# An attention and mixture-of-experts kernel: the same operations in another searched order

## The chip, the cores and the metric

The kernel runs on one core of a Trainium2 chip. The metric is the device time of one execution in microseconds (us); of several executions the median is given. The core has five engines with an instruction stream each: PE (TensorE, matrix products into PSUM), DVE (VectorE), ACT (ScalarE), POOL (GpSimd) and SP (SyncE, which here issues the loads and stores). Transfers between HBM and the on-chip memory are moved by 16 DMA engines that all streams share.

## The reference

The input x holds 4 batches of 11456 tokens with 128 channels. Two attention steps with 32 inducing points give every token a mixture of 32 vectors, and a top-1 mixture of 8 experts follows.

```python
def mab(q, kv):
    s = scale * (q @ kv.transpose(0, 2, 1))
    a = np.exp(s - s.max(-1, keepdims=True))
    a /= a.sum(-1, keepdims=True) + 1e-09
    return a @ kv
h = mab(I, x)          # 32 rows for each batch
x = mab(x, h)          # a mixture of these rows for each token
...
logits = x @ w_gate    # 8 experts, the largest is taken
h = np.maximum(xe @ w1[e], 0.0)
out[mask] = gate_w[mask, None] * (h @ w2[e])
```

## The kernel before

A batch is cut into 6 groups, so there are 24 tiles of 960 KB, numbered k = 6 x batch + group. A tile is loaded once (LT, L728) and stays on the chip until it has been used twice. The first use belongs to the step that makes h: scores against the inducing points (S1, L740), their largest (M1, L743), exponentials (E1, L780), and the product with the tokens themselves in another layout (H, L793). That layout is either loaded (LN, L731) or made by transposing the tile on PE (TR, L751) and copying it out of PSUM on ACT or DVE (TE, L759 or L761).

When a batch's h is there, one expert is assumed for the whole batch, taken from its mean row. DVE computes the row index of that expert's matrices (pick, L841 to L844), ACT reads the index and fetches both matrices with one transfer of 1 MB (fetch, L852 and L853, names GA0 to GA3). The gate product G (units, L880) and the product P (second, L902) read them and give h4, the 32 output rows of that batch. One buffer holds the matrices, so a fetch waits until P of the batch before has read them.

The second use of a tile: scores against h (S2, L740), exponentials (E2, L981), gate logits of four tiles at a time (LG, L985) with a chain of small DVE operations and one exponential (PR, L1026), spreading of the gate (SP, L1041), weighing (W, L1044), the product with h4 in four quarters (X, L1048), a copy of each quarter out of PSUM on ACT or DVE (V, L759 or L761), and one store of the tile by SP (OUT, L734). The four copies of a tile must be done before its store. Tile 22 is stored in two halves.

At the end a scalar, nleft, is computed (count_left, L1055 to L1060). Every engine reads it (L1164), and only if it isn't zero a general part follows that treats each token by its own expert (not entered here).

The order of all this is not written by hand. `make_plan` lists the operations with what each depends on, the buffers it takes, and a rank; `schedule` (L114 on) plays the engines through in time and gives each free engine the ready operation with the lowest rank. The instructions are then issued in that order, and on the chip each engine keeps to it. The rank of an operation is a sum of three numbers from the table PLAN, and the same table names for some copies the engine (ACT or DVE) that has to make them:

```python
r = plan[table][at] + off.get(what, 0) + own.get(name, 0)
```

The fetch and the store are such operations (w is the buffer of the matrices, ix the pick, vs the four copies of a tile):

```python
ga = gc = op(f"GA{b}", ("C", b, "GA"), {"ACT": (1300, 1300)}, lambda w=w, b=b: K.fetch("ACT", w, b, 0, 2 * F), [ix], take=[w], dma=("ACT", 1048576, 8192, 2400, 1300))
op(f"OUT{name}", ("X", k, "OUT"), {"SP": (400, 400)}, lambda ob=ob, b=b, g=k % NG, lo=lo, hi=hi: K.store(ob, b, g, lo, hi), vs[lo:hi], use=[ob], dma=("SP", P * size, size, 1000, LAG))
```

A tile in memory is one of 19 buffers named big, a bank of PSUM is named bank, and the numbers behind these names in the rows below tell one buffer from another.

Of the kernel before, what the change touches and what calls it, by code (L numbers as in the profile page):

```python
# [19 lines left out]
P = 128  # L20
# [15 lines left out]
SWITCH, STICK, INFLIGHT, BEHIND = 145, 11437, 3, 15731  # L36
# [77 lines left out]
def schedule(ops, caps, groups):  # L114
# [54 lines left out]
    while done < len(ops):  # L169
# [83 lines left out]
        22576, -215, 14169, 28949, 16135, 34517, 14097, 191, 4002, 6426, 7963, -6317, 10900, 1498, 8024, -8116, 8452,  # L253
        -538, 10545, -12557, 2397, -23157, 10591, 16643,
    ],
    "L": [
        -29189, -20072, -22138, -25158, -35332, -21900, -37208, -31064, -25285, -35121, 5583, 8561, 12852, 1863,
        -4529, 16988, 4272, 5407, 14400, 6829, 17850, 29121, 33456, 31071,
    ],
    "N": [  # L260
        12772, 4341, -2376, 6450, 8539, 16120, -6122, -27329, -2958, 18930, -18049, -32917, -14840, 13704, -18266,
        3276, 12274, 10466, -10433, -30560, 12476, 19786, 30172, 37075,
    ],
    "S": [
        10068, 9798, -1298, -1286, -4892, -6897, -23049, -13916, -26910, -16934, -10574, 2427, -23263, -49482, 8229,
        -28059, 34705, -41524, 1858, 4084, 16975, -13970, 16003, 35169,
    ],
    "R": [
        -22198, -46069, -31967, -57874, -57432, 2945, -46313, -34100,
    ],  # L270
    "X": [
        3851, -21673, -61781, 13591, -13346, -23064, -23010, -4543, 1213, -60388, -39796, -45518, -11840, 8412,
        -27893, -41405, -19426, -45032, -29697, 7754, -3754, -15221, -20520, -12592,
    ],
    "C": [
        4574, -20912, -62733, -11069,
    ],
    "off": {
# [7 lines left out]
    },  # L286
    "own": {
# [1101 lines left out]
```

## Time and profile before

| | us |
|---|---|
| median of 3 runs | 163.82 (163.63 to 164.72) |
| the profiled execution, its own time | 162.93 |
| the profiled execution, span from the first to the last instruction | 161.1 |
| PE busy | 142.5 |
| DVE busy | 123.8 |
| ACT busy | 95.7 |
| moved by DMA in the span | 61.74 MB |

Three stages follow each other and overlap: loads (until about 90 us), stores (from about 90 us on), and a last part in which no engine computes while the remaining stores are moved. Times in the rows are counted from the start of the span. A row of the windows gives busy time and, in brackets, the number of instructions of PE, PEld (weight loads), DVE, ACT and POOL, then PE's granted clock, the busy share of the DMA engines and the rate that they moved. The rate and the busy share of the DMA engines have to be read together: an engine counts as busy while a packet is under way, however long it takes.

### The profile page before, as it was taken

To read this page: it belongs to the slowest core of one execution; us is meant where nothing else is said; L and a number is where in the kernel's file an instruction comes from. 1 tells how busy PE (TensorE), PEld (TensorE's weight loads), DVE (VectorE), ACT (ScalarE), POOL (GpSimd) and SP (SyncE) were. 2 spreads that over 40 slices of the span, in tenths; PEclk is the share of its full clock that TensorE was granted. 3 is DMA by queue.
4 is the path that set the end of the run, shared out by engine and by line. 5 is a ranking of instruction groups with operands and counts; after the bars stand their busy time and mean duration, and the time that the engine had idled before them with its cause. 6 is when DMAs were issued, how large, how long until landed. Compare 5 with 4: busy or idle time off the path is not lost.

```text
span 161.1 us, 4956 instructions
## 1 busy us (share of the span) xinstructions
PE 142.5 (89%) x1980; PEld 85.1 (53%) x1981; DVE 123.8 (77%) x351; ACT 95.7 (59%) x197; POOL 10.3 (6%) x59
## 2 busy tenths in 40 slices
PE   7999899999999999999999999999999967994100
PEld 4385665866974753495855764654543232471100
DVE  2046669864969999999999899999999999994000
ACT  3074751725804545796857884896986988667000
POOL 1100000000001011001000011002010000102000
PEclk9999999999999999999999999999999999999555
DMA  5999999999799999999999879999999999999991
GB/s 154 429 420 430 420 422 422 419 417 417 268 375 405 373 422 422 425 415 427 414 430 421 337 320 416 323 369 408 401 350 280 428 423 420 425 427 417 432 371 39
DMA packets 9389, 61.74 MB, mean 383 GB/s; under 512 B 1040, under 2 KB 1168, under 8 KB 8848
## 3 DMA queue, kind: packets, MB, share of 16 engines
q1 hardware_dynamic: 8640, 57.10, 86.7%
q10 hardware_dynamic: 720, 4.26, 7.5%
q8 instruction: 17, 0.28, 0.7%
q14 instruction: 12, 0.10, 0.2%
HBM read 37.76 MB, written 23.59 MB: 381 GB/s over the span
## 4 chain that ended last, share of the span: by engine, by line
PE 76%; DVE 9%; DMA 4%; ACT 2%; issue 1%; POOL 1%; SPq 0%; DVEq 0%
PE bank L740 25%; PE bank L751 15%; PE bank L793 13%; PE bank L1048 13%; DMA big<-in_xT 4%; PE bank L704 3%; PE bank L1041 3%; PE bank L985 3%; DVE mid L1044 2%; ACT big L759 2%; DVE big L761 1%; PE bank L902 1%; PE bank L880 1%; DVE mid L1037 1%; POOL thr_all L968 1%
## 5 line engine op out<-in xcount | busy, mean ns | idle before, releaser
L759 ACT COPY big<-bank 128x480 f32<-128x480 f32 (+2 forms) x121 | 60.2, 594 | 26.7 <-PE bank L751 20.4
L1048 PE MATMUL bank<-mid,h 32*128 32x480 f32 x192 | 32.9, 596 | 2.2 <-DVE mid L1044 1.7
L751 PEld LDWEIGHTS bank<-ident,big 128*128 128x128 f32 x210 | 22.7, 141 | 8.9 <-ACT big L759 3.3
L751 PE MATMUL bank<-ident,big 128*128 128x128 f32 x210 | 26.0, 276 | 0.7 <-ACT big L759 0.7
L740 PE MATMUL bank<-big,csb 128*32 128x480 f32 (+2 forms) x200 | 24.6, 554 | 0.4 <-DMA big<-in_xT 0.4
L793 PE MATMUL bank<-big,mid 128*32 128x129 f32 x720 | 24.5, 274 | 0.0
L743 DVE TENSOR_REDUCE mx<-bank 128x1 f32<-128x480 f32 x24 | 15.4, 651 | 11.4 <-PE bank L740 9.9
L793 PEld LDWEIGHTS bank<-big,mid 128*32 128x32 f32 x720 | 21.3, 110 | 4.6 <-issue 2.9
L1048 PEld LDWEIGHTS bank<-mid,h 32*128 32x128 f32 x192 | 15.6, 183 | 13.5 <-ACT big L759 5.9
L981 ACT ACTIVATE mid<-bank,nb 128x480 f32<-128x480 f32 x24 | 15.4, 661 | 11.6 <-DVE nb L976 6.1
L761 DVE COPY big<-bank 128x480 f32<-128x480 f32 (+2 forms) x31 | 19.4, 649 | 2.9 <-PE bank L751 2.0
L740 PE MATMUL bank<-big,hc 128*32 128x480 f32 x192 | 21.5, 568 | 0.0
L780 ACT ACTIVATE mid<-bank,mx 128x480 f32<-128x480 f32 x24 | 15.1, 662 | 7.0 <-DVE mx L777 4.0
L783 DVE STREAM_TRANSPOSE mid<-mid 128x480 f32<-128x480 f32 x24 | 15.3, 656 | 0.8 <-ACT mid L780 0.7
L972 DVE TENSOR_REDUCE mx<-bank 128x1 f32<-128x480 f32 x24 | 15.1, 642 | 0.1
L1044 DVE TENSOR_TENSOR mid<-mid,bank 128x480 f32<-128x480 f32 x24 | 14.7, 634 | 0.2
L1041 PE MATMUL bank<-mid,sel 32*128 32x480 f32 x48 | 13.7, 594 | 0.0
L740 PEld LDWEIGHTS bank<-big,hc 128*32 128x32 f32 x192 | 6.3, 110 | 8.4 <-issue 6.6
L740 PEld LDWEIGHTS bank<-big,csb 128*32 128x32 f32 x200 | 5.9, 110 | 6.4 <-issue 3.0
L1041 PEld LDWEIGHTS bank<-mid,sel 32*128 32x128 f32 x48 | 5.0, 183 | 3.1 <-issue 1.2
L985 PE MATMUL bank<-mid,gzb 128*32 128x480 f32 x48 | 6.0, 570 | 0.0
L700 PE MATMUL bank<-ones 128*128 128x384 f32 x8 | 4.9, 792 | 1.1 <-DVE ones L682 1.1
(100 smaller groups left out, 111.2 us busy)
## 6 DMA issues: line engine op xcount, KB each, us to landing
big<-in_xT SPq DMA_DIRECT2D x23, 960.0 KB, 14.0
out<-big SPq DMA_DIRECT2D x23, 960.0 KB, 7.1
big<-in_xn SPq DMA_DIRECT2D x10, 967.5 KB, 9.9
wt<-in_w ACTq DMA_DIRECT2D x4, 1024.0 KB, 9.8
out<-big SPq DMA_DIRECT2D x2, 480.0 KB, 7.2
big<-in_xT SPq DMA_DIRECT2D x1, 512.0 KB, 3.8
big<-in_xT SPq DMA_DIRECT2D x1, 448.0 KB, 9.8
csb<-in_consts ACTq DMA_DIRECT2D x1, 66.5 KB, 4.0
```

Of the source, the lines that this page charges most:

```text
L740: self.nc.tensor.matmul(self.blk(ps[32 * q : 32 * q + 32, 32 * lo : 32 * hi]), lhsT=lhsT, rhs=x[:, lo:hi, q, :], start=True, stop=True)
L743: self.nc.vector.tensor_reduce(self.mx1[b][g // 2][:, g % 2 : g % 2 + 1], self.bank(fe)[:, :GW], AX.X, ALU.max)
L751: self.nc.tensor.transpose(ps[:, k * P : (k + 1) * P], x[:, k0 + k].rearrange("p q t -> p (q t)"), self.ident)
L759: self.nc.scalar.copy(dst, src)
L761: self.nc.vector.tensor_copy(dst, src)
L780: self.nc.scalar.activation(self.at(e), self.bank(fe)[:, :GW], AF.Exp, bias=self.mx1[b][p + 1][:, 2:3], scale=SCALE)
L783: self.nc.vector.transpose(self.at(e), self.at(e))
L793: self.nc.tensor.matmul(ps[32 * j : 32 * j + 32, : P + 1], lhsT=e[:, k, :], rhs=x[:, k, :], start=(n < 4), stop=(n >= 2 * GB - 4))
L981: self.nc.scalar.activation(self.at(e), self.bank(fe)[:, :GW], AF.Exp, bias=self.nb2[r][:, u : u + 1])
L1041: self.nc.tensor.matmul(self.bank(s)[:, :GW], lhsT=self.sel[rows], rhs=self.at(lv)[rows], start=True, stop=True)
L1044: self.nc.vector.tensor_tensor(out=self.at(e), in0=self.at(e), in1=self.bank(s)[:, :GW], op=ALU.mult)
L1048: self.nc.tensor.matmul(self.bank(o)[:, :GW], lhsT=self.h4[b][rows], rhs=self.at(e)[rows], start=True, stop=True)
```

## The change

The table PLAN has other numbers throughout, two constants of the planner are different, and the lists that fix an engine for some copies are different. The operations, their dependencies, the buffers and the tile sizes are the same. The file grows by 3 lines, so a line number behind the table is 3 higher after the change (L853 is L856).

```diff
-SWITCH, STICK, INFLIGHT, BEHIND = 145, 11437, 3, 15731
+SWITCH, STICK, INFLIGHT, BEHIND = 145, 11302, 3, 13971
...
 PLAN = {
     "A": [
-        22576, -215, 14169, 28949, 16135, 34517, 14097, 191, 4002, 6426, 7963, -6317, 10900, 1498, 8024, -8116, 8452,
+        2385, -1402, 28311, 13134, 33635, 6526, 1078, 21421, 8652, 5804, 12112, -2541, 14024, -7580, 6532, -10203,
...
```

The order was searched with an added charge for stores issued close behind a fetch of expert matrices; that charge is not in the file, only the table that came of it. The lists that fix an engine now name 37 copies for DVE (31 before); in the last stage, behind the logits of tiles 16 to 19, DVE makes 12 copies of outputs where it made 10.

ACT at the fourth fetch (GA3), before the change. The copies of tile 5 go to big_94, those of tile 4 to big_104:

```order
L759 COPY big_95<-bank_79 128x480
L759 COPY big_104<-bank_81 128x480
L759 COPY big_94<-bank_82 128x480
L759 COPY big_94<-bank_84 128x480
L759 COPY big_104<-bank_83 128x480
L759 COPY big_94<-bank_85 128x480
L852 TENSOR_LOAD ii_223
L852 ISA x2
L853 ISA
L853 DMA wt_130<-in_w 128x2048
L759 COPY part_231<-bank_81 128x128
L759 COPY big_104<-bank_86 128x480
```

The same place after the change. Here tile 4 is in big_88 and tile 5 in big_104:

```order
L762 COPY big_88<-bank_85 128x480
L1029 ACTIVATE mid_120<-mid_120 128x60x7
L762 COPY big_104<-bank_84 128x480
L762 COPY big_88<-bank_80 128x480
L762 COPY big_104<-bank_79 128x480
L762 COPY big_104<-bank_86 128x480
L855 TENSOR_LOAD ii_223
L855 ISA x2
L856 ISA
L856 DMA wt_130<-in_w 128x2048
L762 COPY part_231<-bank_81 128x128
L762 COPY big_104<-bank_83 128x480
```

The last copy of tile 4 moved from behind the fetch to ahead of it, with two copies between; the last copy of tile 5 moved from ahead of the fetch to behind it. SP's stores of the two tiles changed places with them.

PE where the gate product of the first pick is made (L704 on csb and hs_208, which the first fetch waits for through DVE), before the change. A row of L740 with hc is the product of scores of one tile in the second use, L793 is one H:

```order
L751 MATMUL bank_83<-ident,big_100 128x128 x3
L740 MATMUL bank_82<-big_99,hc_185 32x480 x4
L704 MATMUL bank_81<-csb,hs_208 32x8 x4
L704 MATMUL bank_81<-csb,hT_all 32x8 x4
L704 MATMUL bank_84<-mq_0_153,fold 32x8 x4
```

The same place after the change:

```order
L754 MATMUL bank_79<-ident,big_99 128x128 x4
L707 MATMUL bank_82<-mq_0_153,fold 32x8 x4
L743 MATMUL bank_81<-big_100,hc_185 32x480 x4
L743 MATMUL bank_85<-big_104,hc_185 32x480 x4
L743 MATMUL bank_84<-big_93,csb 32x480 x4
L743 MATMUL bank_80<-big_94,hc_185 32x480 x4
L743 MATMUL bank_79<-big_87,hc_185 32x480 x4
L796 MATMUL bank_83<-big_95,mid_116 32x129 x15
L707 MATMUL bank_82<-csb,hs_208 32x8 x4
L707 MATMUL bank_82<-csb,hT_all 32x8 x4
```

The pick's products moved behind five products of scores and one H, where they stood behind one product of scores. The user of the fetched matrices, G (L880, now L883), has two products of scores fewer ahead of it than before.

SP at the end, before the change (three full stores behind the two halves of tile 22):

```order
L734 DMA out<-big_90 128x960 x2
L734 DMA out<-big_87 128x1920
L734 DMA out<-big_100 128x1920
L734 DMA out<-big_92 128x1920
L1164 TENSOR_LOAD nleft
```

And after the change:

```order
L737 DMA out<-big_102 128x960 x2
L737 DMA out<-big_93 128x1920
L1167 TENSOR_LOAD nleft
L1167 ISA x2
L737 DMA out<-big_99 128x1920
L737 DMA out<-big_97 128x1920
```

The read of nleft moved from behind all stores to ahead of the last two. On DVE the count (now L1058 to L1063) stands ahead of the last two copies, where it stood behind all of them.

At the start, SP's first transfer is now the whole tile 0; before it was the first half of tile 6, which is now second.

## Rows read from the trace of the kernel before

**Rows 1.** The page, part 2: rate of the DMA engines in 40 slices.
```profile
GB/s 154 429 420 430 420 422 422 419 417 417 268 375 405 373 422 422 425 415 427 414 430 421 337 320 416 323 369 408 401 350 280 428 423 420 425 427 417 432 371 39
```

**Rows 2.** Timeline of the tail, DVE: start us, us, line, operation, idle before.
```profile
148.64 0.17 DVE L1055 TENSOR_TENSOR sure<-low_all,thr_all 128x6 f32<-128x6 f32 x1 [1.24 <-POOL thr_all L968]
...
149.88 0.16 DVE L1060 TENSOR_SCALAR nleft<-bank 128x1 int32<-128x1 f32 x1 [0.68 <-PE bank L1059]
```

**Rows 3.** Windows, two long stretches.
```profile
48.00:124.00 76.00, 76.00 (x1153) 43.34 (x1155) 72.97 (x222) 54.91 (x113) 6.68 (x27) 1.00 0.98 388
124.00:144.00 20.00, 17.29 (x141) 8.12 (x135) 19.44 (x47) 15.53 (x34) 0.70 (x3) 1.00 1.01 424
```

**Rows 4.** DMA issues of 104 to 117.5, 126 to 149, 118.3 to 119.9: KB, us to landing.
```profile
out<-big SPq DMA_DIRECT2D x6, 960.0 KB, 4.7
...
out<-big SPq DMA_DIRECT2D x11, 960.0 KB, 7.4
...
out<-big SPq DMA_DIRECT2D x2, 960.0 KB, 10.8
wt<-in_w ACTq DMA_DIRECT2D x1, 1024.0 KB, 9.7
```

**Rows 5.** Windows around the fourth, the third and the first fetch.
```profile
118.00:120.00 2.00, 2.00 (x36) 0.82 (x28) 1.92 (x6) 1.36 (x4) 0.33 (x2) 1.00 1.04 355
120.00:122.00 2.00, 2.00 (x19) 0.57 (x14) 1.97 (x9) 1.69 (x3) 0.22 (x1) 1.00 0.95 244
122.00:124.00 2.00, 2.00 (x26) 0.69 (x24) 2.00 (x6) 1.56 (x4) 0.00 (x0) 1.00 0.94 239
...
100.00:102.00 2.00, 2.00 (x68) 1.80 (x64) 1.96 (x9) 1.50 (x3) 0.56 (x2) 1.00 1.01 294
102.00:104.00 2.00, 2.00 (x30) 0.88 (x30) 1.93 (x5) 1.44 (x4) 0.00 (x0) 1.00 0.98 393
...
52.00:56.00 4.00, 4.00 (x96) 2.96 (x90) 3.96 (x13) 1.74 (x3) 0.37 (x2) 1.00 0.98 372
```

**Rows 6.** DMA queues in 120 to 123.5; q10 carries the fetches: packets, MB, share.
```profile
q10 hardware_dynamic: 96, 0.79, 92.2%
```

**Rows 7.** Timeline of ACT's and SP's DMA issues at the fourth, third, first fetch.
```profile
118.42 0.35 ACTq L853 DMA_DIRECT2D wt<-in_w  x1
...
118.71 1.18 SPq L734 DMA_DIRECT2D out<-big  x2
...
98.66 0.35 ACTq L853 DMA_DIRECT2D wt<-in_w  x1
...
104.44 0.33 SPq L734 DMA_DIRECT2D out<-big  x1
...
51.91 0.35 ACTq L853 DMA_DIRECT2D wt<-in_w  x1
...
52.10 0.79 SPq L728 DMA_DIRECT2D big<-in_xT  x1
```

**Rows 8.** Timeline of ACT, copies out of PSUM ahead of the fourth fetch.
```profile
112.09 2.41 ACT L759 COPY big<-bank 128x480 f32<-128x480 f32 x5
```

**Rows 9.** DMA in 56 to 60 us: all packets, then the fetches' queue.
```profile
DMA packets 224, 1.67 MB, mean 418 GB/s; under 512 B 14, under 2 KB 14, under 8 KB 111
...
q10 hardware_dynamic: 112, 0.92, 55.2%
```

**Rows 10.** Timeline of PE at the user of the first fetch (L880).
```profile
65.53 1.00 PE L740 MATMUL bank<-big,hc 128*32 128x480 f32 x8
66.33 0.63 PE L880 MATMUL bank<-wt,hT_all 128*32 128x256 f32 x8
```

**Rows 11.** The page, part 5: copies out of PSUM on DVE; busy us, mean ns.
```profile
L761 DVE COPY big<-bank 128x480 f32<-128x480 f32 (+2 forms) x31 | 19.4, 649 | 2.9 <-PE bank L751 2.0
```

**Rows 12.** SP at the end: the last two stores, and the read of nleft.
```profile
147.24 2.31 SPq L734 DMA_DIRECT2D out<-big  x2
...
L1164 SPq TENSOR_LOAD <-nleft x1: 849/849/849, 150.1 to 150.1; - x1
```

More of the change, by code (lines that the diff above doesn't have):

```diff
@@ L252 @@
     "A": [
-        22576, -215, 14169, 28949, 16135, 34517, 14097, 191, 4002, 6426, 7963, -6317, 10900, 1498, 8024, -8116, 8452,
-        -538, 10545, -12557, 2397, -23157, 10591, 16643,
+        2385, -1402, 28311, 13134, 33635, 6526, 1078, 21421, 8652, 5804, 12112, -2541, 14024, -7580, 6532, -10203,
+        7059, -2760, 9977, -13414, 2050, -23025, 10682, 16850,
     ],
     "L": [
-        -29189, -20072, -22138, -25158, -35332, -21900, -37208, -31064, -25285, -35121, 5583, 8561, 12852, 1863,
-        -4529, 16988, 4272, 5407, 14400, 6829, 17850, 29121, 33456, 31071,
+        -29755, -23396, -21084, -25190, -36575, -23093, -34252, -37352, -25092, -31089, 8881, 6270, 12370, -4707,
+        1170, 16463, 3474, 5592, 14308, 6744, 17567, 28569, 32255, 31070,
     ],
     "N": [
-        12772, 4341, -2376, 6450, 8539, 16120, -6122, -27329, -2958, 18930, -18049, -32917, -14840, 13704, -18266,
-        3276, 12274, 10466, -10433, -30560, 12476, 19786, 30172, 37075,
+        -18663, 3735, 12016, 11822, -5651, 15948, 9052, -18534, -11764, 6103, -5977, -35933, -5395, 13660, -27398,
+        17803, 3361, 9450, -16842, -30295, 12619, 20197, 31553, 37979,
     ],
     "S": [
-        10068, 9798, -1298, -1286, -4892, -6897, -23049, -13916, -26910, -16934, -10574, 2427, -23263, -49482, 8229,
-        -28059, 34705, -41524, 1858, 4084, 16975, -13970, 16003, 35169,
+        -280, -4243, -710, 9493, 17027, -7951, -13994, -28002, -24337, 1613, -12108, -17135, -25789, -50709, 7905,
+        -28776, 33975, -41739, 461, -15538, 16653, 3801, 10271, 35050,
     ],
     "R": [
-        -22198, -46069, -31967, -57874, -57432, 2945, -46313, -34100,
+        -44787, -45651, -30899, -58535, -59615, 3019, -22021, -33329,
     ],
     "X": [
-        3851, -21673, -61781, 13591, -13346, -23064, -23010, -4543, 1213, -60388, -39796, -45518, -11840, 8412,
-        -27893, -41405, -19426, -45032, -29697, 7754, -3754, -15221, -20520, -12592,
+        -11971, -2621, -60694, 3686, -13159, -22217, -22667, -4799, -345, -61467, -39936, -46315, -11898, 7638,
+        -17880, -40850, -27968, -46174, -13735, 14632, 7964, -21222, -29646, -19084,
     ],
     "C": [
-        4574, -20912, -62733, -11069,
+        3750, -22440, -63404, -10617,
     ],
     "off": {
[7 rows of a table removed]
[7 rows of a table added]
     },
     "own": {
[133 rows of a table removed]
[134 rows of a table added]
     },
     "ACT": [
[3 rows of a table removed]
[4 rows of a table added]
     ],
     "DVE": [
[3 rows of a table removed]
[4 rows of a table added]
     ],
```

295 rows, old and new, of the table PLAN are left out of this document.

## Prediction

> **What bounds the kernel now.** Read the page first. In its row of rates [rows 1] the DMA engines move 400 to 430 GB/s in most of the 40 slices; the last full number is 371 in slice 39, which ends near 157, and some bytes still move in the last one. The timeline of the tail has the last instruction that an engine computes, nleft, at 149.88 [rows 2], 11 us before the span's end. So the end is a queue of stores that drains, and a microsecond that the DMA engines lose counts whole if nothing fills it later.
>
> Then the long windows [rows 3]. From 48 to 124 us TensorE is busy 76.00 of 76 us and VectorE 72.97: compute sets the pace at which tiles become ready to store. From 124 to 144 the DMA engines run at 424 GB/s; I take that as the full rate.
>
> Then time to landing [rows 4]. The stores of 104 to 117.5 land a median 4.7 us after issue: hardly a queue. Those of 126 to 149 take 7.4, so some 2.7 us of queue stand before them. What built that queue lies between the two: the stores issued at 118.3 to 119.9 need 10.8 us.
>
> The short windows say why [rows 5]: 355 GB/s in 118 to 120, 244 and 239 in the next two. Missing against 424 are 2 x (69 + 180 + 185) = 868 KB, or 2.05 us at the full rate. The engines weren't idle: in 120 to 123.5 us the queue that carries the fetch of an expert's matrices takes 92.2% of their time [rows 6] and moves little in it. The fetch was issued by ACT at 118.42, and SP issued two stores behind it, the first at 118.71, both within 1.18 us [rows 7].
>
> Other fetches cost less. The third, issued at 98.66, has no store behind it until 104.44 [rows 7]; the windows from 100 to 104 show 294 and 393 GB/s [rows 5]: 2 x (130 + 31) = 322 KB or 0.76 us. The first, at 51.91, has one load behind it at 52.10 [rows 7]; 52 to 56 shows 372 [rows 5]: 4 x 52 = 208 KB, 0.49 us.
>
> **The change part by part.** No operation is added or removed: it is the same list, with other ranks, and with other engines for some copies out of PSUM.
>
> *The fourth fetch.* Before, ACT makes the last copy of one tile, issues the fetch, and then makes a small copy and the last copy of another tile: two stores become ready at and behind the fetch. Now the tile whose last copy stood behind the fetch gets it ahead, with two copies between, and only the other tile is completed behind. Copies on ACT go at 0.48 us each (2.41 us for five [rows 8]), so the one store should leave about 1 us ahead of the fetch, and the other about 1.1 us behind it, as the second does today.
> What is this worth? At one end nothing: 2.05 us are lost as before. At the other end the loss becomes that of the first fetch, 0.49. I take 0.76, the third's: it is the nearest in time, with stores around it and not loads, and the dearer of the two. Gain 2.05 - 0.76 = 1.29 us. It reaches the end, since the later stores stand in a queue 2.7 us deep.
>
> Here a rule of the Trainium skill speaks against the change. At 120 to 123.5 the fetch has the engines almost alone [rows 6] and moves 244 and 239 GB/s; at 56 to 60 the first fetch has 55.2% of their time, loads the rest, and 418 GB/s are moved [rows 9]. The page DMA: Bandwidth & Descriptors, section Queues, rings and completion order, says that each engine goes round-robin over the queues that have work, switching at packet boundaries. By that rule alone the bytes would take the same time whichever store stands first, so the sum would be 0 in place of 1.29; the stretch at 56 agrees with it, the one at 120 doesn't. It stands beside the first rival below.
>
> *Evictions before that fetch.* ACT has one exponential fewer ahead of the copies that began at 112.09 [rows 8], and TensorE one product of scores fewer, 0.80 us (from 65.53 to 66.33 [rows 10]). The stores of this stretch stand in no queue, so earlier ones can close small holes. At least 0, at most 0.80 us; copies of another tile come in between, so I take 0.3.
>
> *Copies moved.* VectorE gets two more copies in the last stage, at 649 ns each [rows 11], 1.30 us; ACT two fewer. What hides it is the 2.7 us queue, so I cost it at nothing; without that cover it is 1.30 us.
>
> *The count at the end.* SP now reads the scalar nleft ahead of the last two stores, and VectorE makes the count ahead of its last two copies. Queued behind SP's read are those two stores alone. Today they are issued from 147.24, over 2.31 us, so until 149.55 [rows 12]. At worst they come 1.30 (copies) + 1.40 (the count, 148.64 to 150.04 [rows 2]) + 0.85 (the read [rows 12]) later: 153.1. The engines now end about 159; with the forecast's gain they would be free for the last two stores (1.97 MB, 4.6 us at 424 GB/s) near 153. A store needs some 2.4 of its 4.7 us besides its transfer, so the worst case loses about 2.4 us, the best nothing. I take nothing: the count stands beside copies, and ACT is ahead by what VectorE takes over.
>
> *The start and the first fetch.* The first transfer is now a whole tile rather than the first half of another; TensorE has its warm-up until either can begin. I cost it at nothing, 0.3 us either way. The first gate product comes later on TensorE, and with it the first fetch. I cost that at nothing too; its price is the last rival's.
>
> Sum: 1.29 + 0.3 = 1.6 us. The profiled execution took 162.93 us, its span 161.1; that gives 161.3 for it. The median of the runs is 163.82, 0.9 above it; the same 1.6 off gives 162.2, my forecast.
>
> **The rivals.**
> *No change.* The low rate belongs to the fetch and not to what is issued near it. For it: the stores behind the fetch moved almost nothing in the bad stretch, so it isn't plain how they hurt. Against it: the first and the third fetch, of the same size, lost 0.49 and 0.76. Time: 163.82 - 0.3 = 163.5. The worst case of the count at the end, which gives the gain back, also ends near here.
> *More than forecast.* The fetch and both stores run at the full rate, and small holes close, as far as the queue of 2.7 us lets a gain through. For it: the queue is deeper than the loss that the windows show. Against it: each fetch whose rate I looked up cost something. 163.82 - 2.7 = 161.1.
> *Slower.* The first fetch comes into TensorE's path. It was issued at 51.91 [rows 7]; four products of scores at 0.80 and one sum of about that length now stand ahead of its row index, which makes it 55.9. A fetch lands 9.7 us later [rows 4], at 65.6. Its user, the product at 66.33 [rows 10], has two products fewer ahead of it, so it wants the matrices at 64.7 and is already 0.9 us late. If the low rate comes with any transfer near a fetch, the first loses 2.05 in place of 0.49 and lands at 67.2, 2.5 us late, on an engine without idle time until 124 [rows 3]; and the fourth gains nothing. 163.82 + 2.5 - 0.3 = 166.0. It decides from a lateness of 1.6 us on; below that the fourth fetch's gain outweighs it. Against it: VectorE, which works on what TensorE makes, has 3 us of idle time in that stretch [rows 3] to make good.
>
> **How the numbers follow.** Forecast 0.50, more than forecast 0.16, no change 0.20, slower 0.14. A measurement of this kernel can tell about 1% from no change, 1.64 us: faster is below 162.18, slower above 165.46. The forecast, with half a microsecond of doubt either way, lies on that bound: 0.26 of it counts as faster, 0.24 as within 1%. More than forecast is faster, 0.16; no change is within 1%, 0.20. Of the slower case 0.11 is over 1%, the rest a smaller lateness within it. That makes faster 0.42, within 1% 0.47, slower 0.11. The range goes from 160.6 (half a microsecond beyond "more than forecast") to 164.8, which takes in no change and a smaller lateness of the first fetch; the forecast's own range is 161.3 to 163.1.
>
> **What would show it.** Right: one store issued ahead of the fourth fetch and one about 1 us behind it; the windows that stood at 244 and 239 GB/s above 330; the two stores next to the fetch landing in under 9 us; the stores of 126 to 149 in about 6 us rather than 7.4. Wrong: the fetch again alone on the engines below 300 GB/s; TensorE idle before the product that reads the first fetch; the last two stores issued later than 152 with none in flight before them.

## The result and the profile after

| | before | after |
|---|---|---|
| median of 20 runs each, us | 163.88 | 164.09 |
| ratio, with its 95% interval | 1 | 1.0053 (1.0032 to 1.0073) |
| the profiled execution, us | 162.93 | 163.72 |
| its span, us | 161.1 | 161.8 |

The changed kernel is 0.5% slower by the ratio, some 0.9 us, where 162.2 us had been forecast. The medians of all runs lie only 0.2 us apart; the ratio and its interval are taken over the runs in the faster of two states, and the text goes by them. The number lies in the range; the direction is wrong.

**The fourth fetch went as forecast.** ACT's and SP's DMA issues there (timeline of the changed kernel; its line numbers are 3 higher) answer to [rows 7]:

```profile
118.70 0.33 SPq L737 DMA_DIRECT2D out<-big  x1
...
119.38 0.34 ACTq L856 DMA_DIRECT2D wt<-in_w  x1
...
120.52 0.33 SPq L737 DMA_DIRECT2D out<-big  x1
```

One store leaves 0.7 us ahead of the fetch, one 1.1 us behind it. The windows there, to be read against [rows 5] (last column GB/s):

```profile
118.00:120.00 2.00, 2.00 (x36) 0.96 (x32) 1.93 (x5) 1.83 (x6) 0.01 (x1) 1.00 1.03 416
120.00:122.00 2.00, 2.00 (x28) 0.65 (x20) 1.93 (x7) 1.80 (x4) 0.22 (x1) 1.00 1.00 407
122.00:124.00 2.00, 2.00 (x22) 0.43 (x10) 1.97 (x8) 1.08 (x2) 0.00 (x0) 1.00 1.02 328
```

Missing against 424 GB/s are 2 x (8 + 17 + 96) = 242 KB, 0.57 us, where it was 2.05. Two of the signs that had been named were missed: the window of 122 to 124 stands at 328 and not above 330, and the store behind the fetch landed after 10.1 us and not under 9. The stores of 126 to 149 land after a median 5.9 us in place of 7.4 [rows 4]:

```profile
out<-big SPq DMA_DIRECT2D x9, 960.0 KB, 5.9
```

**The first fetch came into TensorE's path.** PE's timeline at the product that reads it, before in [rows 10]; in brackets the idle time and what ended it:

```profile
63.96 1.02 PE L988 MATMUL bank<-mid,gzb 128*32 128x480 f32 x8
66.38 0.64 PE L883 MATMUL bank<-wt,hT_all 128*32 128x256 f32 x8 [1.40 <-DMA wt<-in_w]
```

The fetch was issued at 56.24 (51.91 before [rows 7]) and needed 10.1 us (ACT's timeline, then the list of DMA issues):

```profile
56.24 0.36 ACTq L856 DMA_DIRECT2D wt<-in_w  x1
...
wt<-in_w ACTq DMA_DIRECT2D x1, 1024.0 KB, 10.1
```

TensorE, which had no idle time in this stretch before, waits 1.40 us. From there on compute is late. The first weighing of a tile, on DVE, of the kernel before and of the changed one:

```profile
81.30 1.18 DVE L1044 TENSOR_TENSOR mid<-mid,bank 128x480 f32<-128x480 f32 x2
```

```profile
82.94 0.61 DVE L1047 TENSOR_TENSOR mid<-mid,bank 128x480 f32<-128x480 f32 x1
```

That is 1.64 us. What the DMA engines moved shows the balance. Three windows of the kernel before, then of the changed one (last column GB/s):

```profile
0.00:56.00 56.00, 53.79 (x820) 36.54 (x825) 36.32 (x98) 24.75 (x49) 2.99 (x25) 1.00 0.95 383
...
56.00:112.00 56.00, 56.00 (x904) 33.36 (x896) 53.57 (x167) 40.70 (x85) 4.83 (x20) 1.00 0.97 397
112.00:128.00 16.00, 16.00 (x141) 6.66 (x136) 15.26 (x42) 13.83 (x31) 0.70 (x3) 1.00 0.99 363
```

```profile
0.00:56.00 56.00, 54.66 (x821) 36.13 (x826) 38.80 (x103) 23.01 (x44) 2.42 (x23) 1.00 0.95 379
...
56.00:112.00 56.00, 54.60 (x890) 31.97 (x879) 52.09 (x158) 39.49 (x85) 5.17 (x21) 1.00 0.95 386
112.00:128.00 16.00, 16.00 (x143) 7.01 (x144) 15.51 (x45) 13.28 (x28) 0.94 (x4) 1.00 1.01 405
```

From 112 to 128 the changed kernel moves 16 x 42 = 672 KB more: 1.58 us gained. By 112 it has moved 56 x 4 + 56 x 11 = 840 KB less: 1.98 us lost. In the page's row of rates most of the loss is one hole, at slice 24:

```profile
GB/s 142 414 427 427 414 425 424 417 417 423 266 387 359 359 423 417 433 423 422 420 421 409 342 158 399 314 409 422 420 412 376 419 425 420 427 427 410 418 369 23
```

The loads are done there, and the first stores wait for compute (slice 24: 158, before 320 [rows 1]; some 650 of the 840 KB). Around 104 to 117 hardly a queue of stores stands (a median 4.7 us to landing before [rows 4], 5.7 after), so what has been moved by 112 is what compute had delivered. In this trace, then, compute that is 1.64 us late costs the DMA engines 1.98 us. Gain and loss leave 0.4 us of loss at 128; the spans differ by 0.7, and the rest isn't accounted for.

VectorE has 37 copies out of PSUM where it had 31 [rows 11] (the page, part 5):

```profile
L764 DVE COPY big<-bank 128x480 f32<-128x480 f32 (+2 forms) x37 | 22.8, 640 | 3.3 <-PE bank L754 3.2
```

What the last two of them and the count cost is tried in e10_count_last.

### The profile page after: what moved, and what is told of

It reads as the page before. It is cut to its first block, busy times and chain, and to the rows that moved or that the text cites. A ratio compares the mean times of both kernels' runs of the same rounds, so it can differ in the third digit from the quotient of the medians.

```text
span 161.8 us, 4949 instructions
## 1 busy us (share of the span) xinstructions
PE 143.5 (89%) x1980; PEld 83.9 (52%) x1981; DVE 127.1 (79%) x356; ACT 93.1 (58%) x192; POOL 10.3 (6%) x59
## 4 chain that ended last, share of the span: by engine, by line
## 5 line engine op out<-in xcount | busy, mean ns | idle before, releaser
L762 ACT COPY big<-bank 128x480 f32<-128x480 f32 (+2 forms) x115 | 57.9, 596 | 34.9 <-PE bank L754 27.4
L1051 PE MATMUL bank<-mid,h 32*128 32x480 f32 x192 | 33.5, 600 | 2.1 <-DVE mid L1047 1.3
L764 DVE COPY big<-bank 128x480 f32<-128x480 f32 (+2 forms) x37 | 22.8, 640 | 3.3 <-PE bank L754 3.2
L743 PE MATMUL bank<-big,hc 128*32 128x480 f32 x192 | 22.0, 567 | 0.0
L1044 PE MATMUL bank<-mid,sel 32*128 32x480 f32 x48 | 13.2, 591 | 0.0
L743 PEld LDWEIGHTS bank<-big,hc 128*32 128x32 f32 x192 | 5.8, 110 | 8.2 <-issue 6.2
L703 PE MATMUL bank<-ones 128*128 128x384 f32 x8 | 5.5, 867 | 1.2 <-DVE ones L685 1.2
L1044 PEld LDWEIGHTS bank<-mid,sel 32*128 32x128 f32 x48 | 4.5, 183 | 3.1 <-issue 1.9
```

The source lines that it names most:

```text
L743: self.nc.tensor.matmul(self.blk(ps[32 * q : 32 * q + 32, 32 * lo : 32 * hi]), lhsT=lhsT, rhs=x[:, lo:hi, q, :], start=True, stop=True)
L762: self.nc.scalar.copy(dst, src)
L764: self.nc.vector.tensor_copy(dst, src)
L1044: self.nc.tensor.matmul(self.bank(s)[:, :GW], lhsT=self.sel[rows], rhs=self.at(lv)[rows], start=True, stop=True)
L1051: self.nc.tensor.matmul(self.bank(o)[:, :GW], lhsT=self.h4[b][rows], rhs=self.at(e)[rows], start=True, stop=True)
```

## The experiments

Most kernels take operations out of the finished order and put them ahead of another, and leave all else where it was:

```diff
+def moved(order):
+    for name, before in MOVES:
+        o = next(x for x in order if x.name == name)
+        order.remove(o)
+        order.insert(next((i for i, x in enumerate(order) if x.name == before), len(order)), o)
+    return order
...
-        for o in schedule(make_plan(K, PLAN), CAPS, GROUPS):
+        for o in moved(schedule(make_plan(K, PLAN), CAPS, GROUPS)):
```

The diffs below show MOVES alone. All results:

| kernel | median, us | before beside it | ratio (95%) |
|---|---|---|---|
| e1_early | 163.79 | 163.62 | 1.0030 (0.9994 to 1.0067) |
| e2_store_ahead | 162.71 | 163.62 | 0.9968 (0.9930 to 1.0007) |
| e3_stores_behind | 164.27 | 163.62 | 1.0072 (1.0040 to 1.0103) |
| e5_evict_first | 164.23 | 163.62 | 1.0071 (1.0047 to 1.0095) |
| e4_fetch_late | 164.17 | 163.35 | 1.0052 (1.0019 to 1.0085) |
| e6_early2 | 163.33 | 163.35 | 1.0044 (1.0008 to 1.0080) |
| e7_queue_filled | 162.91 | 163.35 | 0.9983 (0.9954 to 1.0013) |
| e8_queue_dry | 165.90 | 163.35 | 1.0144 (1.0075 to 1.0213) |
| e9_early3 | 163.81 | 163.49 | 1.0034 (1.0002 to 1.0067) |
| e10_count_last | 164.33 | 163.49 | 1.0064 (1.0034 to 1.0093) |
| e11_both_pieces | 163.69 | 163.49 | 1.0017 (0.9987 to 1.0047) |
| e12_repaired | 164.33 | 163.49 | 1.0059 (1.0022 to 1.0097) |
| e13_old_start | 162.75 | 163.48 | 0.9991 (0.9959 to 1.0024) |
| e14_new_start | 163.49 | 163.48 | 1.0012 (0.9983 to 1.0041) |
| e15_new_end | 162.32 | 163.48 | 0.9945 (0.9913 to 0.9976) |
| e16_old_end | 165.77 | 163.48 | 1.0151 (1.0103 to 1.0199) |
| e17_product_later | 163.24 | 163.08 | 0.9993 (0.9960 to 1.0027) |
| e18_old_middle | 162.62 | 163.08 | 0.9970 (0.9941 to 0.9999) |

Theory A: the gain at the fourth fetch is real, and the late first fetch took it back. The ratio compares with the runs of before beside it, so ratios are compared, not medians.

### Is the late first fetch the loss?

**e4_fetch_late** puts the lateness into the kernel before.

```diff
+MOVES = (("GA0", "E2.0"),)
```

> The kernel before with one thing changed: ACT issues the first fetch behind five exponentials of the second use, at about 57.8 in place of 51.91, so it lands at 67.5 to 68, where TensorE wants it at 66.33. Nothing else is moved. Theory A (a late first fetch stops TensorE and all compute behind it, and that is paid at the end): TensorE idle for 1.2 to 1.6 us before the product that reads the fetch, the compute late by as much from there on, the time 1.2 to 1.6 us above before, 165.0 to 165.4. Rival (what is lost there is made good by slack before the end): TensorE idle as said, but the time within 0.4 us of before.

PE's timeline:

```profile
67.81 0.42 PE L880 MATMUL bank<-wt,hT_all 128*32 128x256 f32 x4 [1.40 <-DMA wt<-in_w]
```

The same 1.40 us of idle time as in the changed kernel, and 0.52% (0.85 us, 0.3 to 1.4): a late fetch is paid for at the end. It is less than I expected, and the interval doesn't say whether it is paid in full. That the two waits are equal to the hundredth is chance. In the profiled executions of five other kernels whose order is the changed one's up to there, TensorE waits 0.78 (e10_count_last), 0.86 (e3_stores_behind), 1.45 (e5_evict_first), 1.48 (e16_old_end) and 2.26 us (e8_queue_dry).

**e1_early**, **e6_early2** and **e9_early3** make the fetch early in the changed kernel.

```diff
 e1_early
+MOVES = (("cg0", "S2.5"), ("ix0", "M2.5"), ("GA0", "M2.5"))
 e6_early2
+MOVES = (("cg0", "S1.19"), ("ix0", "T1.12"), ("GA0", "T1.12"))
 e9_early3
+MOVES = (("cg0", "S1.19"), ("ix0", "T1.12"), ("GA0", "T1.12"), ("S2.4", "hT1"))
```

> The changed kernel with one thing put back: the row index of the first batch (its gate product on TensorE, its pick on VectorE) and the first fetch that waits for it go ahead of five products on TensorE and of what VectorE does with them. Everything else keeps its order. Theory A (the change lost its gain to the first fetch, which was issued at 56.24, landed at 66.33 and left TensorE idle for 1.40 us before the product that reads it): fetch issued near 52.3, landed near 62, no idle time there, the weighing of the first stores at 81.5 in place of 82.94, and the end 1.4 us earlier: 162.7 us where the changed kernel takes 164.1. Theory B (the compute is late for another reason, or the hole in the DMA traffic at 92 to 98 belongs to the order of the first stores): the wait goes but the first stores leave where they did, time within 0.4 us of the changed kernel.

> As e1_early, but the gate product of the first batch goes one product of scores later than there, since in e1_early TensorE waited 0.28 us ahead of it and the work behind it came 0.6 us late. Theory A (the lateness of the compute is paid in full at the end): fetch issued near 53.3, landed near 63.2, no idle time before its product at 65; the compute, 1.68 us late in the changed kernel and 0.90 in e1_early, is 0.2 to 0.4 late; the time is 1.2 us under the changed kernel's, near 162.8. Rival (the end is set in the last stage, where the count and two more copies stand ahead of the last two stores, and an earlier compute is worth half of itself at most, as in e1_early): 163.4 or more.

> As e6_early2, with one more product of scores ahead of the turn of the second batch's sums, which waited 0.7 us on TensorE there because VectorE made the row index first. Theory A (what the changed kernel lost is the late first fetch): the compute, 1.68 us late in the changed kernel and 1.20 in e6_early2 (0.35 of that from its first 47 us), is 0.1 to 0.6 late, TensorE has no idle time over 0.3 us from 46 to 82, and the time is 0.8 to 1.2 us under the changed kernel's, 163.0, thus below before by 0.2 to 0.5 per cent. Rival (the rest was lost in the last stage): no better than e1_early, 0.2 to 0.4 per cent above before.

None of them came out as theory A said. The wait for the fetch was gone in each, but TensorE waited elsewhere, near the row index that had been moved up. PE's timeline of e1_early at the gate product, and of e9_early3:

```profile
49.94 0.25 PE L707 MATMUL bank<-csb,hs 128*32 128x8 f32 x8 [0.28 <-ACT mid L783]
```

```profile
55.21 0.61 PE L743 MATMUL bank<-big,hc 128*32 128x480 f32 x4 [0.73 <-ACT mid L984]
```

They stayed 0.30 to 0.44% above before, which the intervals don't separate from the changed kernel's 0.53. e9_early3 has the number of its rival (0.2 to 0.4% above); the rival's reason, a loss in the last stage, is answered by e15_new_end below. These three don't decide it: the first weighing is still 0.86 (e1_early) to 1.23 us (e9_early3) late.

### What makes the low rate at the fourth fetch?

**e2_store_ahead** makes the change's rearrangement there in the kernel before, and nothing else.

```diff
+MOVES = (("V4.0", "V5.1"), ("V4.3", "V5.1"), ("OUT4", "V5.1"), ("V5.3", "di2"), ("OUT5", "S2.22"))
```

> The kernel before with the one rearrangement at the fourth fetch alone: of the two tiles whose stores stood at and behind the fetch, one gets its last copies ahead of the other's, so that its store leaves about 0.7 us ahead of the fetch, and only the other store follows, about 1.1 us behind it. Theory A (the stall at the fourth fetch hangs on stores issued close behind it): the windows from 118 to 124 move at least 380 GB/s on average in place of 279, and the time falls by 1.2 to 1.5 us, to 162.5. Rival (the low rate belongs to that fetch or that stretch, whatever is issued near it, and the changed kernel's better windows come from its compute being 1.7 us later): windows and time as before, within 0.3 us.

Windows:

```profile
118.00:120.00 2.00, 2.00 (x28) 0.67 (x24) 1.83 (x5) 1.18 (x4) 0.22 (x1) 1.00 1.06 396
120.00:122.00 2.00, 2.00 (x22) 0.57 (x14) 1.97 (x8) 1.80 (x3) 0.22 (x1) 1.00 0.93 261
122.00:124.00 2.00, 2.00 (x26) 0.69 (x24) 2.00 (x6) 1.45 (x4) 0.00 (x0) 1.00 1.03 412
```

The loss is 2 x (28 + 163 + 12) = 406 KB, 0.96 us in place of 2.05 [rows 5], and the time 0.32% lower, half a microsecond where 1.2 to 1.5 had been expected (the interval reaches from 1.1 us to nothing). The three windows average 356 GB/s, short of the 380 that theory A had named.

**e3_stores_behind** puts both stores behind the fetch again, in the changed kernel. From S2.18 on two PSUM banks change places.

```diff
+MOVES = (("OUT5", "M2.18"), ("V5.0", "V4.3"), ("OUT4", "M2.18"), ("V4.3", "di2"))
```

> The changed kernel with the old arrangement at the fourth fetch: the tile whose store left ahead of the fetch gets its last copy behind it, the other tile is finished just before it, so both stores are issued at and behind the fetch, at about +0.3 and +1.2 us. Two PSUM banks change places from there on, so that no product waits for the later copy. Theory A (the gain at the fourth fetch is real and was offset elsewhere): the windows of 120 to 124 fall from 368 to some 250 GB/s, 1.2 us are lost and the time rises to 165.3. Rival (the stall is not decided by the stores' place): windows and time stay within 0.3 us of the changed kernel's 164.1.

The issues (timelines of ACT and SP) and the windows:

```profile
119.50 0.34 ACTq L856 DMA_DIRECT2D wt<-in_w  x1
...
119.84 1.54 SPq L737 DMA_DIRECT2D out<-big  x2
...
118.00:120.00 2.00, 2.00 (x33) 0.97 (x36) 1.93 (x5) 1.92 (x5) 0.22 (x1) 1.00 1.03 408
120.00:122.00 2.00, 2.00 (x24) 0.65 (x20) 1.93 (x7) 1.80 (x4) 0.23 (x1) 1.00 1.04 363
122.00:124.00 2.00, 2.00 (x22) 0.57 (x14) 1.97 (x7) 1.00 (x3) 0.00 (x0) 1.00 0.90 358
```

Both stores stand behind the fetch, as close as before, and only 0.67 us is lost; the time is 0.2% above the changed kernel's, where theory A had 1.2 us. So the place of these two stores alone isn't the cause, and the sentence of theory A on it falls. A third theory, C: a store behind a fetch is held up whatever happens, and it hurts only if SP's queue has run empty by then. Here the stores ahead (issued at 115.7 and 117.1) were still moving. The queues in 121.5 to 123.5 (q1 is SP's, q10 the fetch's; packets, MB, share of the engines) show both at work:

```profile
q10 hardware_dynamic: 39, 0.32, 50.6%
q1 hardware_dynamic: 62, 0.35, 42.6%
```

**e8_queue_dry** takes the store ahead of them away, by one more move of SP's order.

```diff
+MOVES = (("OUT5", "M2.18"), ("V5.0", "V4.3"), ("OUT4", "M2.18"), ("V4.3", "di2"), ("OUT6", "M2.18"))
```

> As e3_stores_behind (both stores behind the fetch), and the store before them is moved behind them too, in SP's order alone, so that none is issued in the 3 us ahead of the fetch. Theory C (what counts is a store queue that has run empty when the fetch's packets begin): the low rate comes back, under 300 GB/s from 121 to 125 with hardly a packet of a store for 2 us or more after the fetch's first, and the time rises by 1.5 us over e3_stores_behind, to 165.8 (some of it for the empty time ahead of the fetch). Theory A (the place behind the fetch): no worse than e3_stores_behind by more than 0.4 us, since the same two stores stand behind it there.

Issues and windows, then the queues in 121.2 to 124.9:

```profile
120.11 0.34 ACTq L856 DMA_DIRECT2D wt<-in_w  x1
...
120.44 2.14 SPq L737 DMA_DIRECT2D out<-big  x3
...
120.00:122.00 2.00, 2.00 (x28) 0.65 (x20) 2.00 (x8) 1.80 (x4) 0.03 (x1) 1.00 0.65 112
122.00:124.00 2.00, 2.00 (x25) 0.40 (x14) 1.89 (x7) 0.93 (x2) 0.20 (x1) 1.00 0.92 303
124.00:126.00 2.00, 2.00 (x26) 0.68 (x22) 2.00 (x6) 1.86 (x5) 0.00 (x0) 1.00 0.95 286
```

```profile
DMA packets 106, 0.87 MB, mean 235 GB/s; under 512 B 0, under 2 KB 0, under 8 KB 0
...
q10 hardware_dynamic: 106, 0.87, 87.1%
```

All 106 packets are the fetch's. The first of three stores was issued at 120.44, and up to 124.9, 4.5 us later, none of its packets moves (what SP's queue still moved before 121.2 belongs to the store issued at 116.3, which landed at 121.5). At the full rate these 3.7 us would have moved 699 KB more: 1.65 us lost. Ahead of them the queue ran empty, and that costs too. The time is 0.7% above e3_stores_behind (1.2 us), on the side that C named, but with only four runs and intervals of 0.7 and 0.3% that is not clear of the noise, and the profiled execution also waited 1.40 us longer for the first fetch than that of e3_stores_behind. So it is the windows that speak for C, not the time. In the kernel before it looks the same: in 120 to 123.5 the fetch moves 0.79 [rows 6] of 0.84 MB.

**e7_queue_filled** was to fill the queue in the kernel before, with the store ahead of the fetch made later.

```diff
+MOVES = (("V6.1", "V4.0"), ("OUT6", "V4.0"), ("P2", "S2.20"), ("S2.20", "V4.0"))
```

> The kernel before with both stores left where they are, at and behind the fourth fetch (about +0.3 and +1.1 us). What moves is the store before them: one of its copies is made three copies later, so that it leaves near 117.8 in place of 116.34; two products on TensorE change places for its PSUM bank. Theory A (stores issued close behind the fetch cause its low rate): the windows of 120 to 124 stay near 242 GB/s and the time within 0.3 us of before. Theory C (the low rate comes where the store queue has run empty when the fetch's packets begin, as at 120 us before; a store issued 0.6 us ahead of the fetch keeps it filled): those windows rise to 330 GB/s or more and the time falls by 0.8 us or so, as in e2_store_ahead.

It settles half. The fetch left at 117.72 and a store 0.9 us behind it, and yet the rate behind 121 is 405 and 435 GB/s (387 on average from 120 to 124), as theory C said and not theory A. But the queue ran empty ahead of the store that had been made later, the loss came there, 2 x (247 + 141) = 776 KB or 1.83 us in 117 to 121, and the time stayed, as theory A said. C isn't the whole of it either: in 119 to 120 only SP's packets move (31, and the engines count as fully busy), and the rate is 238 GB/s all the same.

```profile
117.00:119.00 2.00, 1.89 (x32) 0.81 (x35) 1.53 (x4) 2.00 (x6) 0.48 (x2) 1.00 0.52 177
119.00:121.00 2.00, 2.00 (x28) 0.64 (x22) 1.83 (x5) 0.56 (x2) 0.22 (x1) 1.00 0.97 283
121.00:123.00 2.00, 2.00 (x26) 0.51 (x22) 1.97 (x10) 1.53 (x4) 0.00 (x0) 1.00 0.98 405
123.00:125.00 2.00, 2.00 (x27) 0.95 (x22) 2.00 (x4) 1.32 (x3) 0.00 (x0) 1.00 1.05 435
```

### The first stores and the end

**e5_evict_first**, in the changed kernel:

```diff
+MOVES = (("V0.1", "V3.1"), ("V0.2", "V3.1"), ("OUT0", "V3.1"))
```

> The changed kernel with the four copies of its second output tile made one after the other, ahead of the copies of the third tile that stand between them now; the second store should leave near 94.3 in place of 95.83. Theory A (all compute is 1.7 us late because of the first fetch, and the hole in the DMA traffic at 92 to 98 follows from that): only what this store itself gains, 0 to 0.6 us, since the third store leaves no earlier. Theory B (the hole is made by the order of these copies): the windows of 94 to 96 rise from 46 to 350 GB/s or so and the time falls by 1.3 us or more.

No gain: the hole went from 92 to 96 (200 to 296 GB/s) to 100 to 108, where the changed kernel moves 361 and 355:

```profile
92.00:96.00 4.00, 3.72 (x98) 2.52 (x94) 3.80 (x11) 3.49 (x10) 0.60 (x3) 1.00 0.72 296
...
100.00:104.00 4.00, 4.00 (x80) 2.10 (x76) 3.77 (x11) 1.85 (x5) 0.56 (x2) 1.00 0.86 288
104.00:108.00 4.00, 4.00 (x62) 2.34 (x54) 3.81 (x12) 3.33 (x7) 0.24 (x1) 1.00 0.64 264
```

So another order of these copies only moves the hole; that it is set by what compute has delivered fits this, but wasn't tried by itself.

**e10_count_last** and **e12_repaired** (the moves of e9_early3 and this one):

```diff
+MOVES = (("LEFT", "end"),)
```

> The changed kernel with the count placed last: VectorE makes its last two copies ahead of the count, and SP issues the last two stores ahead of its read of the count's scalar (as before the change). Theory D (the count ahead of the last two stores costs at the end): those stores leave near 148.5 and 149.7 in place of 150.50 and 150.94 and the time falls by 0.3 to 0.8 us. Theory A (the queue of stores that stands before them hides it): they leave earlier, and land when they did; time within 0.3 us of the changed kernel.

> e9_early3 and e10_count_last together: the changed kernel with the early first fetch and the count behind the last stores. Theory A: as e9_early3 within 0.3 us. Theory D: 0.3 to 0.8 us under e9_early3, and the fastest of the kernels so far, near 162.5.

The last two stores of the changed kernel, then of e10_count_last: SP's timeline, and the issues with the time to landing.

```profile
150.50 1.54 SPq L737 DMA_DIRECT2D out<-big  x2
...
out<-big SPq DMA_DIRECT2D x2, 960.0 KB, 8.1
```

```profile
149.40 1.63 SPq L737 DMA_DIRECT2D out<-big  x2
...
out<-big SPq DMA_DIRECT2D x2, 960.0 KB, 9.7
```

They leave 1.1 us earlier and need 1.6 us more. The queue hides the count, as theory A said; nothing is gained (1.0064 beside the changed kernel's 1.0053). e12_repaired agrees with e9_early3 within the intervals.

### Start, middle and end exchanged

**e11_both_pieces** has the moves of e2_store_ahead and e4_fetch_late together, in the kernel before.

> The kernel before with the two pieces put into it that the changed kernel is thought to consist of: one store ahead of the fourth fetch (as in e2_store_ahead, 0.3 per cent under before) and the first fetch issued near 57.9 (as in e4_fetch_late, 0.5 per cent above). Theory A (gain and loss add up): 0 to 0.4 per cent above before, the windows of 120 to 124 at 330 GB/s or more, TensorE idle for 1.3 to 1.6 us at 66. Rival (the late compute changes what is queued at the fourth fetch, so the pieces don't add): under before by 0.2 per cent or more, or above by 0.7 or more.

1.0017: the two pieces about add up (0.9968 and 1.0052 give 1.0020).

In e13 to e16 and e18, `schedule` takes for each engine the next name of a list (and each copy goes to the engine on whose list it stands):

```diff
-                if o.ready[e] > t or (e == "DVE" and "ACT" in o.dur and busy["ACT"] - t <= BEHIND):
+                if o.ready[e] > t or o.name != LISTS[e][at[e]]:
```

The lists are the orders of the two kernels, cut where each engine has done the same operations in both: near 57 and near 100 us.

| start | middle | end | kernel |
|---|---|---|---|
| old | old | old | before |
| old | new | new | e13_old_start |
| new | old | old | e14_new_start |
| old | old | new | e15_new_end |
| new | new | old | e16_old_end |
| new | old | new | e18_old_middle |
| new | new | new | the changed kernel |

> Each engine's order taken from the kernel before up to 57 us (at that point every engine has done the same operations in both kernels) and from the changed kernel from there on. Theory A (the start of the changed order, with its late first fetch, is the loss): first fetch at 51.9, no idle time of TensorE before its product, compute within 0.3 us of before at 82 and at 124, the fourth fetch as in the changed kernel, and the time 0.3 to 0.6 per cent below before, near 163.0 (where e2_store_ahead was). Rival (the changed order of the middle or the end costs by itself): no idle time either, but the time 0.2 per cent above before or more.

> The reverse: the changed kernel's order up to 57 us, that of the kernel before from there on. Theory A: first fetch at 56.2, TensorE idle for 1.2 to 1.6 us at 65 to 66, compute 1.4 to 1.7 us late, the stall at the fourth fetch as before or somewhat smaller, and the time 0.5 to 0.9 per cent above before (as e4_fetch_late, 0.5). Rival (middle or end): idle time as said, but under 0.3 per cent above before.

> The order of the kernel before up to 100 us and the changed kernel's from there on: what the change does at the fourth fetch and in the last stage, with nothing of its start. Theory A: 0.3 to 0.6 per cent below before, like e2_store_ahead; windows of 120 to 124 at 330 GB/s or more. Rival (the changed end costs what its fetch gains): within 0.1 per cent of before or slower, though the windows are better.

> The reverse: the changed kernel's order up to 100 us, that of the kernel before from there on. Theory A: late by 1.7 us at 82 as the changed kernel, without its gain at the fourth fetch: 0.6 to 1.0 per cent above before. Rival (the loss is in the changed end): no slower than the changed kernel (0.5 per cent above before) or faster than it.

The end: new against old it brings 0.55% behind the old start and middle (e15_new_end), and 0.98% behind the new ones (1.0151 to 1.0053). The windows of 112 to 128, e15_new_end and then e16_old_end, are close to those of the changed kernel (405) and of before (363):

```profile
112.00:128.00 16.00, 16.00 (x140) 6.68 (x140) 15.27 (x43) 13.78 (x29) 0.94 (x4) 1.00 1.01 399
```

```profile
112.00:128.00 16.00, 16.00 (x148) 7.08 (x143) 15.47 (x44) 13.22 (x28) 1.15 (x5) 1.00 1.00 369
```

Start and middle: together they cost 1.1% (0.9945 to 1.0053) or, with the old end, 1.5% (1 to 1.0151), more than theory A had for e16_old_end. But the new start alone costs 0.1% (e14_new_start), though its fetch is as late (56.41), where theory A had 0.5 to 0.9. PE's timeline of e14_new_start says why (L941 is the product that reads the fetch):

```profile
66.27 1.02 PE L801 MATMUL bank<-big,hc 128*32 128x480 f32 x8
67.08 0.64 PE L941 MATMUL bank<-wt,hT_all 128*32 128x256 f32 x8
```

It doesn't wait. In the old middle two products of scores stand ahead of it that the new middle has behind it.

The new middle behind the old start, e13_old_start, hit neither theory: 0.9991 (0.9959 to 1.0024), where theory A had 0.3 to 0.6% below before and the rival 0.2% above. Its fetch leaves at 52.00 and TensorE doesn't wait for it. Yet it is 0.46% above e15_new_end, which is barely clear of the noise: the new middle seems to cost something without that wait too.

**e17_product_later** moves that one product, **e18_old_middle** the whole middle.

```diff
 e17_product_later
+MOVES = (("G0", "TR15.3"),)
```

> The changed kernel with one product moved: the one that reads the first fetch stands behind the two products of scores that follow it now, which is where the kernel before has it. The fetch stays late (56.2, landed 66.4). Theory A (the loss is the product's wait for the fetch): it starts near 66.6 without idle time before it, compute at 82 and at 124 is 0.2 to 0.7 late in place of 1.7, the gain of the fourth fetch stays, and the time is 0.1 to 0.5 per cent below before. Rival (VectorE then waits for that product as long as TensorE did, so the lateness stays): idle time gone, lateness at 82 over 1.2 us, time 0.3 per cent above before or more.

> The changed kernel with the order of the kernel before from 57 to 100 us: late first fetch, but its product two products later, the first stores in the old order, and the changed end. Theory A: as e17_product_later, 0.2 to 0.5 per cent below before. Rival (the late first fetch costs through something else than that product, so that the changed start spoils the gain whatever follows): 0.2 per cent above before or more.

PE's timeline of e17_product_later:

```profile
66.83 0.64 PE L883 MATMUL bank<-wt,hT_all 128*32 128x256 f32 x8
```

One product moved by two places takes the wait away, and with it 0.60% (1.0053 to 0.9993, with some 0.4% either way), 1.0 us; the old middle as a whole takes 0.83%. Theory A had 0.1 to 0.5% below before for the one, which is missed by a hair, and 0.2 to 0.5 for the other. So about half of the 1.1% is the wait: a fetch 4.3 us later together with a user 1.6 us earlier, neither of which makes TensorE wait for it by itself (e14_new_start, e13_old_start). The lateness of the first weighing isn't the whole price: it comes at 81.77 in e17_product_later and at 82.48 in e18_old_middle, which is no slower. The rest isn't settled: e17_product_later is still 0.5% above e15_new_end, and with intervals of 0.3% either way the runs don't tell which operations of the new middle and start cost it.

The fastest is **e15_new_end**: the kernel before up to 100 us, the changed one from there, 0.55% (0.24 to 0.87) faster than before and so faster than both.

## Why the prediction was wrong

- *The fourth fetch*, 1.29 us: right in its direction and nearly in size. The windows give 2.05 - 0.57 = 1.48 us; from 112 to 128 it is 1.58. The exchanged ends bring 0.55 to 0.98%, 0.9 to 1.6 us of time. Its reason, what is issued around a fetch, was half right: two stores behind the fetch cost little while stores ahead of them are still moving (0.67 us, e3_stores_behind) and much where the queue has run dry (e8_queue_dry). Why is open.
- The first rival, *No change*, asked how stores that move almost nothing can hurt. They are held up for 4.5 us (e8_queue_dry), and the fetch by itself doesn't reach the full rate though the engines count as busy: by an estimate from the rows one of its packets takes 0.49 us there (87.1% of 16 engines' 3.7 us, 106 packets) and 0.32 us beside loads (55.2% of 16 engines' 4 us, 112 packets [rows 9]). The rule of the Trainium skill that was weighed there (DMA: Bandwidth & Descriptors, section Queues, rings and completion order) speaks of queues that have work. In e3_stores_behind both had, and shared the engines (50.6 and 42.6%); in e8_queue_dry SP's moved nothing until 124.9, and whether it had work for the engines by then no run shows.
- *Evictions before that fetch*, 0.3 us: nothing of it is seen in the time. The fetch is 0.96 us later than before and the first weighing 1.64, so 0.7 us was made up on the way; whether any of it reached the end isn't shown.
- *Copies moved* and *the count*, nothing: right for the count (e10_count_last); the moved copies weren't tried alone.
- *The start and the first fetch*: "I cost that at nothing too" is the step that failed. The runs show a wait of 1.40 us in its place; e17_product_later takes it away, and 0.60%, 1.0 us, with it. The rival had its numbers: issue at 55.9 (56.24), 9.7 us to landing (10.1), wanted at 64.7 (64.98), 0.9 us late at least (1.40). What was wrong in it is its "Against": VectorE's idle time made nothing good, since TensorE itself has no idle time until 124 [rows 3], and the weighing behind the wait stayed 1.64 us late. And "it decides from a lateness of 1.6 us on" set a wait of 1.4 us beside a gain of 1.6 as if nothing else were lost on the way; the exchanges show that something is (e17_product_later, without the wait, is still 0.5% above e15_new_end). The rival's own case, 2.5 us late, no gain at the fourth fetch and 166.0, did not come: what came is the smaller lateness below 1.6 us that it had called outweighed. A mechanism whose price I had worked out on an engine without idle time stood with a chance of 0.14 beside a sum in which it cost nothing.
- The size of the first fetch's own loss, 0.49 us, was misread: the dip of 52 to 56 [rows 5] is there in the changed kernel too, where the fetch is issued only at 56.24, and behind it the rate is full:

```profile
52.00:56.00 4.00, 4.00 (x109) 2.58 (x105) 3.83 (x17) 1.76 (x3) 0.59 (x2) 1.00 0.95 331
56.00:60.00 4.00, 4.00 (x92) 2.48 (x85) 3.72 (x16) 2.19 (x6) 0.94 (x4) 1.00 1.02 426
```

## What to carry to other kernels

Where two streams of work meet at a transfer, follow the transfer's landing and its user's place in one sum: here each could move by some microseconds without a wait, and both together stopped an engine that has no slack. Late compute was paid for where the DMA queue ran empty later, so a gain in the DMA's last stretch is compared with what compute lost ahead of that point. Of a new order that brings one gain, exchange the parts at points where every engine has done the same work; here the end alone was worth 0.55%, and the whole cost 0.53%.

## What was not expected of the hardware

A store issued 0.33 us behind a fetch, with SP's queue run nearly empty, moved no packet for 4.5 us (e8_queue_dry: issued at 120.44, only the fetch's packets until 124.9), while the fetch alone moved 235 GB/s against 424 for full traffic. The same pair of transfers with stores still in the queue cost 0.67 us instead of the 2.05 of the kernel before (e3_stores_behind). Why the store waits so long was not tried.
